# DeltaNet with a GELU MLP: the triangular inverse by 16-row blocks on GpSimd, four-tile products, and planned instruction refills

## The chip, the core and the metric

The kernel runs on one core of one Trainium2 chip. The metric is the device time of a whole execution in microseconds (us), the median of three runs. Five engines work side by side, each through its own list of instructions in order, and tell each other by semaphores when a result is there: TensorE (PE) multiplies matrices, VectorE (DVE) and ScalarE (ACT) work element by element, GpSimd (POOL) does so[...], and SyncE (SP) here only issues transfers (DMA). PE results land in PSUM, which has eight banks here; everything else lies in SBUF, 128 partitions wide.

## What is computed

First a delta-rule recurrence for 4 batches x 8 heads, 768 steps, head width 48; then an MLP on the 3,072 rows of 384 that come out of it.

```python
def _attn_ref(q, k, v, beta):
    k_n = k / (np.linalg.norm(k, axis=-1, keepdims=True) + 1e-06)
    state = np.zeros((B, H, D, D))
    for t in range(S):                       # S = 768
        kt, vt, bt = k_n[:, :, t], v[:, :, t], beta[:, :, t, None]
        y[:, :, t] = einsum('bhd,bhde->bhe', q[:, :, t], state)
        v_old = einsum('bhde,bhd->bhe', state, kt)
        state = state + bt[..., None] * einsum('bhd,bhe->bhde', kt, vt - v_old)
    return y
# x = y as rows (b, s) of all heads: 3072 x 384
h = x @ w_in                                 # 384 -> 2048
g = 0.5 * h * (1 + tanh(c * (h + 0.044715 * h**3)))
return g @ w_out                             # 2048 -> 384
```

A kernel can't afford 768 steps in a row. It takes the sequence in 12 chunks of 64 steps. Inside a chunk the updates depend on each other through a 64x64 triangular matrix per head: with K the normalized keys and N the strictly triangular part of the Gram matrix K K^T scaled by beta, the chunk needs T = (I + N)^-1. Then R = V - K S (S is the state at the chunk's start), U = beta T R, the output is Q S + tri(Q K^T) U, and the next state is S + K^T U. Only this last part runs from chunk to chunk; T of a chunk needs nothing but its keys and beta.

## The kernel before

The program lists operations with their costs and dependencies, a planner in the kernel orders them for each engine when the program is built, and the order is fixed from then on. So what lies beside what is decided by the planner, not by the order of the text. Two heads share the 128 partitions, 16 pairs make the 32 heads; `g` is one of two groups of eight pairs.

```python
def prep(c):                     # ... norms of the keys of chunk c
    sq = k*k; ss = sum(sq)       # POOL or ACT, then DVE
    sr = ss ** 0.5               # ACT Sqrt for c < 3, else POOL pow
    rn = 1/(sr + 1e-6)           # DVE
    KQ[:, 0] = kf * rn           # POOL
    KQ[:, 1] = qf                # POOL or ACT
    KQT = dma_transpose(KQ)      # SP: keys and queries, head width on the partitions
```

(The lines above are shortened to what they do; those below are code, with cuts.)

```python
def intra(c, g):
    def gd():                                     # Gram: K K^T and K Q^T, four tiles
        for mm in range(4):
            for (hh, a) in ((0, 0), (1, 1), (0, 1), (1, 0)):
                ...
                r.append((bank(h, hh)[cc, 128*mm:128*mm+128], KQT[i][rr, 0, m, cc], KQT[i][rr, :, m, cc], ...))
    ... # N = Gram * (mask * beta)   DVE from PSUM;   DT = K Q^T * mask   DVE from PSUM
    ... # W = I + N, Z = I - N       POOL (DVE for c < 2)
    def prod(hx, lhs, rhs):
        def body():
            return [(bank(hx)[64*a:64*a+64, 64*p:64*p+64], lhs[64*a:64*a+64, p, :],
                     rhs[64*a:64*a+64, p, :], True, True, True) for p in range(8) for a in range(2)]
        return f_mms(body)
    ... # X = W^T by 16 PE transposes, evacuated by ACT
    for j in range(5):                            # Newton: Z <- Z (2I - X Z)
        op(..., {"pe": prod(h1, Zo, X)}, ...)
        op(..., {"dve": f_tt(F, bc(twoI), v1(h1), ALU.subtract)}, ...)
        op(..., {"pe": prod(h2, F, Zo)}, ...)
        op(..., {"act": f_act(dst, v1(h2))}, ...)  # last round writes TT

def state(c):
    ... # qs: Q S;  ks: K S                   PE, 32 products each, four tiles
    ... # R = vf - K S                        DVE
    def tr():                                 # T R: 32 products, tile (a, a): two of four tiles
        return [(bank(h2, p//8)[64*a:64*a+64, ...], TT[i][64*a:64*a+64, p, :],
                 R[64*a:64*a+64, p, :], True, True, True) for p in range(NP) for a in range(2)]
    ... # U = beta * T R                      DVE
    ... # ku: K^T U, S = S + K^T U            PE four tiles, DVE
    ... # du: tri(K Q^T) U, added to Q S in PSUM   PE, two tiles
    ... # x = output, two evacuations         ACT

def mlp(t):                                   # tiles of chunks: [0] [1,2] [3,4] ... [11]
    op({"sp": 1.1}, {"sp": f_dma(xT[...], x[...], True)}, ...)     # transposing DMA
    for fc in range(FC):                      # 16 slices of the hidden width
        ... # m1: 3 products, w columns (512, or 256 for one chunk);  gT = gelu   ACT
    for u in range(w // 128):
        ... # m2: 16 products of 384 columns;  osb = PSUM   DVE or ACT;  DMA out
```

Of the kernel before, what the change touches and what calls it, by code (L numbers as in the profile page):

```python
# [6 lines left out]
BF16 = mybir.dt.bfloat16  # L7
ALU = mybir.AluOpType
# [3 lines left out]
C = 64  # L12
# [3 lines left out]
KEEP = 0.0  # L16
BANKS = {"t": (0, 6), "f": (6, 8), "l": (0, 8)}
NEAR = {"pe": 0.3, "dve": 0.05, "act": 0.05, "pool": 0.0, "sp": 0.0}


class Op:
    __slots__ = ("idx", "cost", "fns", "deps", "prio", "alloc", "uses", "dma", "lat",
                 "eng", "start", "end", "count", "clock", "sync", "mode", "bw")


class Plan:
# [14 lines left out]
    def op(self, cost, fns, reads=(), writes=(), prio=0.0, alloc=(), dma=None, lat=0.0, mode="t", bw=0.0):  # L41
        o = Op()
        o.idx = len(self.ops)
        o.cost, o.fns, o.prio, o.dma, o.lat, o.mode, o.bw = cost, fns, prio, dma, lat, mode, bw
        o.alloc = tuple(alloc)
        o.sync = set()
# [8 lines left out]
        for b in writes:  # L55
            if b in self.last_w:
                deps.add(self.last_w[b])
            deps.update(self.readers.get(b, ()))
# [14 lines left out]
    def schedule(self):  # L73
# [16 lines left out]
        pe_mode = "t"  # L90
        dma_free = 0.0
# [5 lines left out]
        def dep_time(o, e):  # L97
            t = 0.0
            for d in o.deps:
                p = ops[d]  # L100
                t = max(t, p.end + (p.lat if p.dma else (0.03 if p.eng == e == "pe" else LAT[p.eng])))
            return t
# [16 lines left out]
        while n_left:  # L119
            pick = None  # L120
            for e in ENGINES:
# [3 lines left out]
                for i in ready[e]:  # L125
# [4 lines left out]
                    bb = []  # L130
                    if o.alloc:
                        ok = True
                        taken = []
                        for h, n in o.alloc:
                            sv = [(k, bank_free[k]) for k in taken]
                            for k in taken:
                                bank_free[k] = None
                            f = find_banks(n, t, *BANKS[o.mode])
                            for k, x in sv:
                                bank_free[k] = x  # L140
                            if f is None:
                                ok = False
                                break
                            bb.append((h, f[1], n))
                            taken += list(range(f[1], f[1] + n))
                            t = max(t, f[2] + 0.15)
                        if not ok:
                            continue
                    late = max(0.0, t - free_at[e])
                    pr = o.prio  # L150
                    if e == "pe" and (o.mode == "t") != (pe_mode == "t"):
                        pr += KEEP
                    far = late > NEAR[e]
                    key = (far, t if far else 0.0, pr, i)
                    if best is None or key < best[0]:
                        best = (key, i, t, bb)
# [6 lines left out]
            _, i, t, bb, e = pick  # L163
            o = ops[i]
            if e == "pe" and (o.mode == "t") != (pe_mode == "t"):
                t += SWITCH
                pe_mode = o.mode
            o.eng, o.start, o.end = e, t, t + o.cost[e]
            if o.dma:
                dma_free = max(o.end + 1.3, dma_free) + o.bw  # L170
                o.lat = dma_free + 0.5 - o.end
# [28 lines left out]
    def emit(self):  # L200
# [21 lines left out]
        for _ in range(len(ops)):  # L222
# [12 lines left out]
            for d in o.deps | o.sync:  # L235
                p = ops[d]
                if p.eng == "pe" and e == "pe" and not p.dma:
# [45 lines left out]

def f_tt(out, a, b, op):
# [27 lines left out]
def d_ps(n):  # L312
    return {"dve": 0.13 + 1.07e-3 * n}


def d_any(n):
    return {"act": 0.18 + 0.83e-3 * n, "dve": 0.13 + 1.07e-3 * n}
# [6 lines left out]
def d_pool2(n):  # L324
    return {"pool": 0.10 + 2.0e-3 * n}


def bass_deltanet__then__act_gelu_tanh_kernel(
# [12 lines left out]
    NP = NH // 2  # L341
    NCH = S // C
    KT = DM // 128
    FC = FF // 128
    TILES = [[0]] + [[c, c + 1] for c in range(1, NCH - 1, 2)] + [[NCH - 1]]
# [7 lines left out]
    with nc.allow_non_contiguous_dma("head rows"), nc.allow_low_precision("bf16 matmuls"):  # L353
# [3 lines left out]

        identF = sb("identF", [128, 128], F32)
        mU128 = sb("mU128", [128, 128], F32)
        idI = sb("idI", [128, 64], F32)  # L360
        mU = sb("mU", [128, 64], F32)
        half = sb("half", [128, NP], F32)
        BL = sb("BL", [128, 3, 2, 64], F32)
        bcol = sb("bcol", [128, NP, NCH], F32)
        RL, RB, NSQ = 3, 3, 3
        identB = sb("identB", [128, 64], BF16)
        twoI = sb("twoI", [128, 64], BF16)
        kf = [sb(f"kf{i}", [128, NP, D], F32) for i in range(RL)]
        qf = [sb(f"qf{i}", [128, NP, D], F32) for i in range(RL)]
        vf = [sb(f"vf{i}", [128, NP, D], F32) for i in range(RL)]  # L370
        sq = [sb(f"sq{i}", [128, NP, D], F32) for i in range(2)]
        ss = [sb(f"ss{i}", [128, NP], F32) for i in range(2)]
        sr = [sb(f"sr{i}", [128, NP], F32) for i in range(2)]
        rn = [sb(f"rn{i}", [128, NP], F32) for i in range(2)]
        KQ = [sb(f"KQ{i}", [128, 2, NP, 64], BF16) for i in range(RB)]
        KQT = [sb(f"KQT{i}", [128, 2, NP // 2, 128], BF16) for i in range(RB)]
        NU = [sb(f"NU{i}", [128, NP, C], F32) for i in range(2)]

        def ring(nm, n, w):
            return [[[sb(f"{nm}{i}{g}{j}", [128, 8, w], BF16) for j in range(n)] for g in range(2)] for i in range(RB)]  # L380

        Nb, Wb, Xb, Zb, Fb = ring("N", 1, C), ring("W", 1, C), ring("X", 1, C), ring("Z", 2, C), ring("F", 1, C)
        DTb = [sb(f"DT{i}", [128, NP, C], BF16) for i in range(RB)]
        TT = [sb(f"TT{i}", [128, NP, C], BF16) for i in range(RB)]
        Rb = [sb(f"R{i}", [128, NP, D], BF16) for i in range(2)]
        Ub = [sb(f"U{i}", [128, NP, D], BF16) for i in range(2)]
        Sb = [sb(f"S{i}", [128, NP, D], BF16) for i in range(2)]
        x = sb("x", [128, 2, B, DM], BF16)
        xT = sb("xT", [128, 2, B * KT, 128], BF16)
        W1 = sb("W1", [128, KT, FF], BF16)  # L390
        W2 = sb("W2", [128, FC, DM], BF16)
        gT = [sb(f"gT{i}", [128, FC, 512], BF16) for i in range(2)]
# [16 lines left out]

        def aff(dst, cmp_, fill, pat, cm):  # L410
            return lambda g: g.affine_select(out=dst, in_=dst, compare_op=cmp_, fill=fill, base=0,
# [6 lines left out]
        op({"dve": 0.1}, {"dve": lambda e: e.memset(half[:, :], 0.5)}, writes=["half"], prio=-100)  # L418
        for i in range(RB):
            op({"dve": 0.7}, {"dve": lambda e, i=i: e.memset(KQ[i][:, :, :, D:64], 0.0)},  # L420
               writes=[f"KQz{i}"], prio=-90 + i)
        const("identF", identF, 0.0, ALU.not_equal, 1.0, [[-1, 128]], 1)
        const("mU128", mU128, 1.0, ALU.is_gt, 0.0, [[1, 128]], -1)
        for nm, big, sm in (("idI", identF, idI), ("mU", mU128, mU)):
            bn = {"mU": "mU128", "idI": "identF"}[nm]
            for a in range(2):
                r = slice(64 * a, 64 * a + 64)
                op({"dve": 0.1}, {"dve": f_cp(sm[r, :], big[r, r])}, reads=[bn], writes=[nm + str(a)], prio=-80)
        MASKU, IDI = ["mU0", "mU1"], ["idI0", "idI1"]
        op({"dve": 0.1}, {"dve": f_cp(identB[:, :], idI[:, :])}, reads=IDI, writes=["identB"], prio=-80)  # L430
        op({"dve": 0.1}, {"dve": lambda e: e.tensor_scalar(twoI[:, :], idI[:, :], 2.0, None, op0=ALU.mult)},
           reads=IDI, writes=["twoI"], prio=-80)

        bulk = []

        def gate():
            return bulk[-2] if len(bulk) > 1 else []

        def load(nm, c, pr):
            t, src = {"kf": (kf, k), "qf": (qf, q), "vf": (vf, v)}[nm]  # L440
            s = c % RL
            sv = src.rearrange("b h s d -> (b h) s d").rearrange("(p a) s d -> a s p d", a=2)
            after = gate()
            for a in range(2):
                op({"sp": 0.65}, {"sp": f_dma(t[s][64 * a:64 * a + 64, :, :], sv[a, C * c:C * c + C, :, :])},
                   reads=after, writes=[f"{nm}{s}_{a}"], prio=pr, dma=f"d_{nm}{c}", bw=1.05)
            bulk.append([f"{nm}{s}_{a}" for a in range(2)])

        w1v = moe_w_in.rearrange("(kt p) f -> p kt f", p=128)
        w2v = moe_w_out.rearrange("(fc p) e -> p fc e", p=128)  # L450

        def load_w(nm, j, pr):
            if nm == "W1":
                dst, src, bw = W1[:, j, :], w1v[:, j, :], 2.9
            else:
                dst, src, bw = W2[:, 4 * j:4 * j + 4, :], w2v[:, 4 * j:4 * j + 4, :], 2.2
            op({"pool": 0.8}, {"pool": f_dma(dst, src)}, reads=gate(), writes=[f"{nm}{j}"], prio=pr,
               dma=f"d_{nm}{j}", bw=bw)
            bulk.append([f"{nm}{j}"])

        STEP = 28.0
# [5 lines left out]
        load("kf", 0, -70)  # L467
        for dup in range(2):
            op({"sp": 0.65}, {"sp": f_dma(BL[:, :, dup, :], bfl)}, writes=[f"BL{dup}"], prio=-69, dma="d_BL", bw=0.4)
        load("qf", 0, -68)  # L470
        load("kf", 1, -67)
        load("qf", 1, -66)
        W1N = [f"W1{kt}" for kt in range(KT)]
        W2N = [f"W2{j}" for j in range(4)]

# [7 lines left out]
        op({"pe": 1.0}, {"pe": f_mms(bt_mms)}, mode="f", reads=["BL0", "BL1", "identF"], writes=[hb_ + (0,), hb_ + (1,)], alloc=[(hb_, 1)], prio=-50)  # L483
        for a in range(2):
            r = slice(64 * a, 64 * a + 64)
            op({"dve": 0.35}, {"dve": f_cp(bcol[r, :, :], lambda a=a, r=r: bank(hb_)[r, 0:NH * NCH].rearrange(
                "q (p a c) -> q p a c", a=2, c=NCH)[:, :, a, :])}, reads=[hb_ + (a,)], writes=[f"bcol{a}"], prio=-49)
        BCOL = ["bcol0", "bcol1"]


        def prep(c):
            s, i, j = c % RL, c % RB, c % 2
            pr = T(c, -STEP)
            kn = [f"kf{s}_0", f"kf{s}_1"]
            parts = [slice(0, 8), slice(8, 16)] if c == 0 else [slice(0, NP)]
            for n, u in enumerate(parts):
# [3 lines left out]
                op(cost, {"pool": f_tt(sq[j][:, u, :], kf[s][:, u, :], kf[s][:, u, :], ALU.mult),  # L500
# [314 lines left out]
```

## Time and profile before

| What | Value |
|---|---|
| Time, median of 3 | 326.49 us (325.32 to 327.86) |
| Profiled span, first to last instruction | 322.0 us |
| PE busy | 272.2 us, 7,158 products |
| DVE, ACT, POOL busy | 175.0, 175.3, 127.1 us |
| Solver products X,Z and Z,F, 64x64 | 1,920 and 1,920 |
| MLP products of 512, 256 and 384 columns | 240, 96 and 384 |
| DVE, F out of PSUM, 120 times | 80.4 us, 684 ns each |
| POOL, square roots by pow, 9 times | 26.2 us, 2,911 ns each |
| Transfers | 31.84 MB in 116,206 packets, 110,640 of them under 512 bytes |
| Mean granted PE clock | 0.945 of full |

How to read it: a row of the profile names the engine, the operation, the output and inputs by the program's names, how often it ran, its busy time and the mean of one. "ps" is any PSUM tile, so "ps<-X,Z" is the first product of a solver round and "ps<-Z,F" the second; "ps<-xT,W" and "ps<-W,gT" are the MLP's two layers. "L301" is only the helper that emits products. Products overlap in PE's pipeline, and the profile's end of a product is modelled; the start of the next one is measured. "issue" in the chain is time in which an engine waited for nothing that the profile shows. q8 is the queue that brings instructions.

### The profile page before, as it was taken

The numbers are of one execution on the slowest core, as the hardware profiler recorded it, in microseconds if no ns is written. First come the engines' busy times: TensorE is split into PE (matmuls) and PEld (weight loads), VectorE is DVE, ScalarE is ACT, GpSimd is POOL, SyncE is SP. The second block draws the span as 40 slices with busy tenths as digits, with TensorE's granted clock in tenths as the row PEclk, the third lists the DMA queues.
The fourth block names the chain that finished last, engine by engine and source line by source line (L and its number), as shares of the span: only waits on it lengthen the run. The fifth ranks groups of instructions, "written<-read, shape, count | busy, mean of one in ns | idle before, by whom it ended". The sixth has DMA issues, their size and how long they took to land.

```text
span 322.0 us, 15234 instructions
## 1 busy us (share of the span) xinstructions
PE 272.2 (85%) x7158; PEld 178.4 (55%) x7158; DVE 175.0 (54%) x279; ACT 175.3 (54%) x309; POOL 127.1 (39%) x96
## 2 busy tenths in 40 slices
PE   1158745988859789999899979989999999989995
PEld 1147644656636466666556556555566556544662
DVE  3489723767557467766775566674556554320111
ACT  4325543668447578634778443777345774168330
POOL 2842330877987257455546371260202211000000
PEclk9998775779998799999999999999999999999999
DMA  7998889879998435495557541709001002101022
GB/s 134 168 182 169 131 119 180 155 151 172 170 176 139 93 69 102 85 181 111 111 100 107 113 103 51 118 4 118 26 29 53 2 9 48 66 36 24 24 75 49
DMA packets 116206, 31.84 MB, mean 99 GB/s; under 512 B 110640, under 2 KB 115760, under 8 KB 116144
## 3 DMA queue, kind: packets, MB, share of 16 engines
q1 hardware_dynamic: 113600, 27.73, 45.5%
q0 software_dynamic: 2544, 3.15, 6.8%
q8 instruction: 56, 0.92, 1.2%
q14 instruction: 6, 0.05, 0.0%
HBM read 20.64 MB, written 4.72 MB: 79 GB/s over the span
## 4 chain that ended last, share of the span: by engine, by line
PE 51%; DMA 22%; issue 7%; DVE 7%; ACT 5%; SPq 4%; POOL 2%; POOLq 0%
PE ps L301 50%; DMA kf<-in_k_dram 8%; DMA qf<-in_q_dram 6%; DMA vf<-in_v_dram 4%; SPq L309 4%; DMA xT<-x 2%; DVE F L285 2%; DMA KQT<-KQ 1%; ACT Z L294 1%; ACT sq L294 1%; ACT x L294 1%; PE ps L600 1%; POOL sr L285 1%; DVE ss L503 1%; DVE R L285 1%
## 5 line engine op out<-in xcount | busy, mean ns | idle before, releaser
L285 DVE TENSOR_TENSOR F<-twoI,ps 128x512 bf16<-128x512 bf16 x120 | 80.4, 684 | 58.4 <-PE ps L301 57.7
L301 PE MATMUL ps<-xT,W 128*128 128x512 bf16 (+1 forms) x336 | 80.6, 364 | 1.8 <-ACT gT L294 1.0
L294 ACT ACTIVATE Z<-ps 128x512 bf16<-128x512 f32 x96 | 56.2, 595 | 42.3 <-PE ps L301 41.5
L294 ACT ACTIVATE gT<-ps 128x512 bf16<-128x512 f32 (+1 forms) x112 | 58.2, 536 | 32.3 <-PE ps L301 31.2
L301 PE MATMUL ps<-W,gT 128*128 128x384 bf16 x384 | 70.0, 327 | 0.6 <-ACT gT L294 0.6
L301 PE MATMUL ps<-X,Z 64*64 64x64 bf16 x1920 | 53.9, 201 | 12.8 <-ACT Z L294 6.9
L301 PE MATMUL ps<-Z,F 64*64 64x64 bf16 x1920 | 54.7, 201 | 8.7 <-DVE F L285 4.0
L301 PEld LDWEIGHTS ps<-X,Z 64*64 64x64 bf16 x1920 | 42.8, 116 | 29.8 <-ACT Z L294 15.1
L301 PEld LDWEIGHTS ps<-Z,F 64*64 64x64 bf16 x1920 | 43.0, 115 | 28.7 <-DVE F L285 15.8
L285 POOL TENSOR_TENSOR W<-identB,N 128x512 bf16<-128x512 bf16 x20 | 23.0, 1151 | 81.8 <-DVE N L285 78.1
L301 PEld LDWEIGHTS ps<-W,gT 128*128 128x128 bf16 x384 | 34.5, 98 | 21.8 <-ACT gT L294 0.8
L301 PEld LDWEIGHTS ps<-xT,W 128*128 128x128 bf16 x336 | 26.7, 100 | 23.1 <-ACT gT L294 4.2
L290 DVE COPY osb<-ps 128x384 f32<-128x384 f32 x20 | 11.1, 557 | 41.3 <-PE ps L301 41.3
L285 POOL TENSOR_TENSOR sr<-ss,half 128x16 f32<-128x16 f32 x9 | 26.2, 2911 | 5.4 <-DVE ss L503 5.2
L285 POOL TENSOR_TENSOR KQ<-kf,rn 128x768 bf16<-128x768 f32 (+1 forms) x12 | 17.1, 1423 | 21.2 <-PE ps L301 16.9
L285 POOL TENSOR_TENSOR NU<-mU,bcol 128x1024 f32<-128x1024 f32 x12 | 23.6, 1971 | 4.4 <-DVE N L285 4.0
L294 ACT ACTIVATE x<-ps 64x768 bf16<-64x768 f32 x24 | 19.3, 804 | 8.2 <-PE ps L301 7.9
L285 POOL TENSOR_TENSOR Z<-identB,N 128x512 bf16<-128x512 bf16 x20 | 23.0, 1151 | 0.0
L294 ACT ACTIVATE TT<-ps 128x512 bf16<-128x512 f32 x24 | 14.3, 596 | 13.4 <-PE ps L301 13.4
L294 ACT ACTIVATE X<-ps 128x512 bf16<-128x512 bf16 x24 | 14.3, 595 | 12.9 <-PE ps L600 12.9
L285 DVE TENSOR_TENSOR N<-ps,NU 128x512 bf16<-128x512 f32 x24 | 16.3, 686 | 8.6 <-PE ps L301 8.6
L301 PE MATMUL ps<-KQT 48*64 48x128 bf16 x384 | 12.7, 246 | 6.6 <-DMA KQT<-KQ 6.4
(49 smaller groups left out, 202.4 us busy)
## 6 DMA issues: line engine op xcount, KB each, us to landing
kf<-in_k_dram SPq DMA_DIRECT2D x24, 192.0 KB, 4.0
qf<-in_q_dram SPq DMA_DIRECT2D x24, 192.0 KB, 3.9
vf<-in_v_dram SPq DMA_DIRECT2D x24, 192.0 KB, 4.3
out_dram<-osb SPq DMA_DIRECT2D x20, 192.0 KB, 1.9
W<-in_moe_w_in_dram POOLq DMA_DIRECT2D x3, 512.0 KB, 6.0
W<-in_moe_w_out_dram POOLq DMA_DIRECT2D x4, 384.0 KB, 7.1
out_dram<-osb SPq DMA_DIRECT2D x8, 96.0 KB, 2.7
BL<-in_beta_dram SPq DMA_DIRECT2D x2, 96.0 KB, 3.6
```

Of the source, the lines that this page charges most:

```text
L285: return lambda e: e.tensor_tensor(out() if callable(out) else out, a() if callable(a) else a, b() if callable(b) else b, op)
L290: return lambda e: e.tensor_copy(out, a() if callable(a) else a)
L294: return lambda e: e.activation(out, a() if callable(a) else a, func)
L301: ins = t.matmul(out, lhsT, rhs, start=st, stop=sp_, skip_group_check=skip)
L309: return lambda e: e.dma_start(out, a)
L503: op({"dve": 0.95 * w}, {"dve": lambda e, u=u: e.tensor_reduce(ss[j][:, u], sq[j][:, u, :], AX.X, ALU.add)}, reads=[f"sq{j}{n}"], writes=[ ...
L600: ins = t.transpose(bankb()[r, p, :], W[r, p, :], identB[r, :])
```

## The change

The new kernel computes the same with another way to T, other layouts, and another planner.

- **T by blocks.** A 64x64 triangle is cut into four 16-row blocks. PE first forms only the four 16x16 diagonal blocks of each Gram matrix (`own`, 64 products of 32x32 per chunk); a DVE transpose brings them to a layout in which each partition holds whole 16x16 blocks, for two chunks at once (a unit). POOL solves them there by substitution: 14 steps of one multiply and one add on short rows (`blocks`; the first unit on DVE). Two DVE transposes return the blocks. `inverse` expands them to block-diagonal matrices (DI, WB), forms E from the Gram matrix and WB in one set of products, and fills the off-diagonal blocks of T in three rounds of products (48, 32, 16 columns). This replaces the 22 sets of 16 solver products and transposes per chunk.
- **All four PE tiles.** In `state`, T R and the product with DT are laid out so that neighbouring products use all four 64x64 tiles (from chunk 2 on for T R). The output comes out transposed, so the MLP's input no longer needs the transposing DMA; rows of the fourth slice are moved by small SBUF to SBUF transfers, and tile 0 uses a fourth weight slice W4 instead.
- **Transposes of K and Q** are done on PE (128 columns each) and evacuated by DVE or ACT. Queries are loaded for two chunks at a time in longer runs.
- **Norms** from chunk 4 on by three Newton steps on DVE, for two chunks together, in place of POOL's pow.
- **MLP tiles** are [0], [1], and then pairs. Weights are loaded by ten POOL-issued transfers for the first layer, behind POOL's start-up work, and four for the second.
- **The planner** models the refill of PE's instructions in blocks of 256 and places bursts so that a refill has time to arrive; priorities are set by a table.

The core of the diff, with cuts:

```diff
+class Fetch:
+    BLOCK, FIRST, EVENTS = 256, 63, 1.0025
+    TIMES = ((50.0, 6.5), (125.0, 4.5), (1e9, 3.7))
+    ...
+                    if e == "pe":
+                        t0 = t + turn(pe_mode, o.mode)
+                        w = o.cost[e] * (COLD if t0 < COLD_T else 1.0)
+                        stall = fetch.run(t0, w, o.nm) - t0 - w
+                        t += max(0.0, stall - SLACK)
...
-    TILES = [[0]] + [[c, c + 1] for c in range(1, NCH - 1, 2)] + [[NCH - 1]]
+    TILES = [[0], [1]] + [[c, c + 1] for c in range(2, NCH, 2)]
...
-            op({"sp": 1.1}, {"sp": f_dma(KQT[i]..., KQ[i]..., True)}, ...)
+                        for m in ms:
+                            ins = e.transpose(tb()[:, m, :], t[:, 2 * m:2 * m + 2, :]..., identB[:, :])
...
+        def own(cs):
+            ...
+                                o = bank(h, hh)[64 * a + 32 * b:64 * a + 32 * b + 32, x_:x_ + 32]
+                                kk = kqt[64 * hh:64 * hh + D, 0, m, a, b, :]
+                                r.append((o, kk, kk, True, True, True))
+        def blocks(cs):
+            eng = "pool" if u else "dve"
+            ...
+            op({"dve": 1.4}, {"dve": lambda e: e.transpose(Tt[j]..., banks2(h)...)}, ...)
+            for s in range(14, 0, -1):
+                w = 15 - s
+                ... # tmp[j, u] = Y[s, u] * Y[j, s]   for w x s elements, two chunks
+                ... # Y[s+1:, 0:s] += tmp
+            ... # XW[0] = Y * beta by rows, XW[1] = Y * beta by columns
+                op({"dve": 1.05}, {"dve": lambda e, w=w: e.transpose(TB1... if w else TB0..., XW[w]...)}, ...)
+        def inverse(c, hs):
+            exp(1, WB[e_], f"WB{e_}", 0)          # DVE (ACT early)
+            exp(0, DI[r_], f"DI{r_}", 0.1)
+            ... # ps = G WB (32 products);  ET = ps * mask
+            for k in (1, 2, 3):
+                n = 64 - 16 * k
+                ... # ps = ET^T src, 32 products of n columns;  TT[:, 16k:] = ps + DI   DVE
-            for j in range(5):
-                ... # Z <- Z (2I - X Z)
...
-                return [(bank(h2, p // 8)[64 * a:64 * a + 64, ...], TT[i][64 * a:64 * a + 64, p, :], ...)]
+                if fl:
+                    return [(bank(h2, p % 2)[HALF[a], D * (p // 2):D * (p // 2) + D],
+                             TT[r_][HALF[a ^ (p % 2)], p, :], R[HALF[a ^ (p % 2)], p, :], True, True, True)
+                            for p in range(NP) for a in range(2)]
+                    r.append((oc(m, hh, a), U[HALF[a], p, :], DTb[r_][HALF[a], p, :], c == 0 and n < 4, True, True))
...
-            op({"sp": 1.1}, {"sp": f_dma(xT[:, s, :, 0:n], x[0:n, s, :, :]..., True)}, ...)
+            for c_ in range(2):
+                for j in range(KT if t else 0):
+                    op({XQ: 0.7}, {XQ: f_dma(xs[64*c_+48:64*c_+64, j, :, 0:n], xs[64*c_+16*j:64*c_+16*j+16, 3, :, 0:n])}, ...)
```

On PE the program order falls from 7,158 products to 5,443; 120 F operations on DVE and 96 Z evacuations on ACT are gone.

## The prediction

> **What bounds the kernel now.** I read the page's busy shares first, then the chain that ended last, then the timeline of TensorE in a steady stretch, because only start-to-start times there tell what a burst of small products really costs.
>
> ```profile
> PE 272.2 (85%) x7158; PEld 178.4 (55%) x7158; DVE 175.0 (54%) x279; ACT 175.3 (54%) x309; POOL 127.1 (39%) x96
> ...
> q8 instruction: 56, 0.92, 1.2%
> ```
>
> TensorE (PE) is the nearest to full; no other engine passes 55%. But 272.2 us is a union of spans whose ends are modelled (201 ns for a 64x64 product that is followed some 16 ns later by the next), so part of it is drain and not work. The chain, in order of time, shows two different kernels:
>
> ```profile
> 10.23 4.70 DMA KQT<-KQ
> ...
> 42.37 4.00 issue
> ...
> 49.25 7.49 DMA xT<-x
> 56.79 1.38 PE ps L301 x13
> ...
> 292.61 25.56 PE ps L301 x165
> ```
>
> Up to 56.8 us it is a latency chain: load, norm, a transposing DMA (4.7 us), five solver rounds of chunk 0, another transposing DMA (7.5 us); only then can the MLP feed PE. Loads stand on the chain again from 87 us (qf 5.00 us, then kf 5.49). The last 26 us are pure MLP. Between, PE is the bound. Its real prices stand in the timeline of the PE rows:
>
> ```profile
> 257.62 0.82 PE L301 MATMUL ps<-xT,W 128*128 128x512 bf16 x3
> 258.37 0.44 PE L301 MATMUL ps<-X,Z 64*64 64x64 bf16 x16
> 258.74 0.82 PE L301 MATMUL ps<-xT,W 128*128 128x512 bf16 x3
> 259.60 0.44 PE L301 MATMUL ps<-Z,F 64*64 64x64 bf16 x16
> 259.87 0.66 PE L301 MATMUL ps<-R,TT 64*64 64x48 bf16 x32
> ...
> 261.59 0.44 PE L301 MATMUL ps<-U,KQ 64*64 64x48 bf16 x32
> 261.86 0.66 PE L301 MATMUL ps<-U,DT 64*64 64x48 bf16 x32
> ...
> 298.79 1.46 PE L301 MATMUL ps<-W,gT 128*128 128x384 bf16 x8
> 300.09 0.49 PE L301 MATMUL ps<-xT,W 128*128 128x256 bf16 x3
> 300.42 1.46 PE L301 MATMUL ps<-W,gT 128*128 128x384 bf16 x8
> ```
>
> Sixteen Z,F products on the two diagonal tiles take 259.87-259.60 = 0.27 us, 17 ns each. Thirty-two U,KQ products on all four tiles take 261.86-261.59 = 0.27 us, 8.4 ns each. U,DT (two tiles, 32), where nothing waits, runs from 62.65 to the next burst at 63.16: 0.51 us, 16 ns, which I use for two tiles. Eight second-layer products take 1.30 us, 162 ns; three 256-column ones 0.33 us, 110 ns; by columns a 512-column one is 217 ns. Three of those are 0.65 us and the small burst starts 0.75 us later: some 0.09 us for a change between MLP and small products.
>
> Sum before: MLP 240x0.217 + 96x0.110 + 384x0.1625 = 125 us. Attention per chunk: 352 solver products and transposes x 16 ns = 5.6; Gram 32x16 ns = 0.5; S,KQT 64x8.4 ns = 0.5; R,TT and U,DT 0.5 each; U,KQ 0.27; together 7.9, times 12 = 95 us. The program order has 224 changes between MLP and small products, x 0.09 = 20 us. Total 240 us, against a PE that ends at 318. So about 78 us is not work: 43 us before 56.8 us (14 of work there), and 35 us after.
>
> In the stretch 112 to 288 us alone the PE groups give 190 and 256 MLP products and 3,744 attention products: 82.8 + 62 + some 15 of changes = 160 of 176 us, 91%.
>
> **The Trainium skill.** "TensorEngine Tiling (Array Packing)", Tiling Modes: 64x64 gives four independent tiles, 32x32 sixteen, and a change of mode drains the array. The trace agrees with both (8.4 against 16 ns; 0.09 us per change). "TensorE: Matmul & The Clock Gate", the aside on 56 ns in Part 1: matmul start-to-start never falls below about 25 ns; the trace differs (8.4 ns on four tiles), and I use the trace. "Runtime: NRT & Kernel Launch", Instruction fetch mechanics: instructions are refilled in blocks of 256. The q8 row agrees: 56 packets, and 2x7158/256 = 55.9. The page calls the cost mostly hidden; the trace shows single "issue" gaps of 4.00 us. "GPSIMD Engine Reference", Elementwise (about 2.6 cycles per element at 1.2 GHz for two inputs) bears on the solver: it would give 1.66 us for 768 elements; in the trace the KQ<-kf,rn products on POOL take 1,477 ns for 768 elements and 827 ns for 384, which is 0.18 us plus 1.69 ns per element.
>
> **The change, part by part.** (1) PE. Removed per chunk: 352 products (5.6 us). Added per chunk: 64 own-block Gram products of 32x32 (at 8.4 ns, an estimate from the four-tile burst, 0.5); 16 transposes of 128 columns for K and Q (by columns 54 ns, 0.9); WB 32x8.4 ns = 0.27; three block rounds of 32 on two tiles, 96x16 ns = 1.5 at most. R,TT moves from two to four tiles (0.5 to 0.27) and so does U,DT, turned round to 64 columns (0.5 to 0.3). With the Gram 0.5, S,KQT twice 0.27 and U,Kn 0.27 a chunk is 5.1, times 12 = 61 us, against 95. MLP gains 16 products of 256 columns (tile 0 takes four contraction slices): 127. The order shows 150 changes for 224: 13.5 against 20. Total 202 for 240: 38 us less work. PE's instructions fall from 7,158 products to 5,443, so 43 refills instead of 56.
>
> (2) Start. Both transposing DMAs leave the first chain. Mine: keys of chunk 1 land about 8 us; norms, scaling, transposes, evacuation, own blocks to about 14.5 (the keys' norm chain before took 5.58 to 9.94); one transpose on VectorE (DVE) of 1,024 elements 1.3; the solve of unit 0 on DVE: 28 dependent small operations at 0.17 to 0.25 (TENSOR_SCALAR and RECIPROCAL of 128x16) plus a handoff, near 0.28, = 8, and four of 512 elements at 0.69; two transposes back: near 28.5. Expansion and block rounds with their DVE and ScalarE (ACT) steps 5; R to U to the output 3.3: x of chunk 0 near 37. But W1 is issued on GpSimd (POOL) only behind its start-up work, which I sum to about 25 us (KQ-sized operations by the rate above), in ten transfers; weight transfers took 6 to 7 us to land on busy queues (the page's DMA issues), so they land 40 to 44. I take the first MLP product at 41 us, against 57.
>
> (3) The solve in steady state. One unit of two chunks on POOL: 28 operations x 0.18 + 2,240 elements x 1.69 ns = 8.8, three 512-element ones at 1.04, and 5 of scaling, squares and masks: 17 us. PE needs per two chunks 20.8 (MLP) + 10 + 2 = 33. POOL lies beside it. DVE per two chunks: I count 26 us (four 0.95, TT 0.95+0.69+0.42, DT two 0.69, DI and output two 0.56 each, reduction 0.94, transposes and norms 2.6, each per chunk). ACT about 25 with its DMA issues. All below 33, so PE remains the bound.
>
> (4) After 41 us: 202 less the 13.5 done by then is 188.5. The order's end is 72+24 first-layer and 64+64 second-layer products without attention: 42 us, dense as the 25.56 us piece is. The other 146.5 I divide by 0.95: before it was 0.91, but loads, transposes and refills are now more out of the way; 154 us. The granted clock fell to 0.5-0.8 between 32 and 72 us before; I add 2.5 us for such a dip. Last evacuation and output as before, 3.8. Span: 41+154+2.5+42+3.8 = 243.3. Time stood 4.5 us above span (326.49 against 322.0): 248 us.
>
> **Rivals.** *The solve becomes the wait*: 28 dependent POOL operations of maybe 0.5 us each with their handoff would make 25 us a unit, still under 33, but the first POOL unit also stands behind the start-up and weight issues; chunk 2 might come after the MLP of tiles 0 and 1 has run out. For it: long in-order POOL list. Against: 39% busy before, and 3 us pow operations (26.2 us in all) are gone. It would add 5 to 15 us: 253 to 263. *DVE and ACT, filled to 80%, stall PE*: before, DVE waited 57.7 us on PE for F and PE only 23.7 for F, at 54% busy; a fuller engine in order gives 0.88 instead of 0.95: 12 us more, 260. *The dense plan works as planned*: efficiency 0.99, start at 37: 234. *The slack eats it*: PE work falls but the recurrence of chunks binds. A state step is about 5 us (four bursts with drain, 0.95+0.95 on DVE, 0.8 on ACT), 60 us in all, so I give it little.
>
> **Range and chances.** The terms with room are the start (37 to 46) and the efficiency (0.88 to 0.99); together about 234 to 266, so the range is 234 to 263. None of the rivals comes near 320: faster by over 2% 0.97, within 0.02, slower 0.01.
>
> **What would show it.** First x,W product near 41 us; PE products 5,443 and 43 instruction packets; PE start-to-start near 8.4 ns in R,TT and WB; no DMA transpose; POOL under 60% with gaps; the final MLP piece 42 us. Wrong if the first MLP product is after 50 us, if PE idles on POOL or DVE for more than 20 us between 60 and 190 us, if 32x32 products cost well over 8.4 ns, or if "issue" gaps stay near 4 us.

## The result, and the profile after

The changed kernel takes 260.25 us (median of 4 runs, 259.79 to 260.78) against 327.0 us before (4 runs): a ratio of 0.797, 95% interval 0.794 to 0.799. I had predicted 248 us, with 234 to 263 as the range. Measured again at a later time, beside runs 9 to 11, the same kernel took 258.82 us; so between two measurements taken at different times, 1.5 us are not read as a difference.

The page of the changed kernel: busy time by engine, the queue of instruction refills, and the chain that ended last by engine.

```profile
PE 216.8 (84%) x5416; PEld 143.3 (55%) x5446; DVE 160.3 (62%) x288; ACT 145.1 (56%) x244; POOL 127.7 (49%) x234
...
q8 instruction: 42, 0.69, 1.2%
...
PE 41%; POOL 28%; DVE 15%; issue 4%; DMA 4%; SPq 3%; ACT 3%; POOLq 0%
```

PE lost 55 us of busy time (272.2 before) and 1,712 products, counted by their weight loads (7,158 to 5,446; 30 product records are missing after). Refills fell from 56 to 42. POOL, 2% of the chain before, is 28% of it now. The DMA share of the chain fell from 22% to 4%: the transposing transfers, 3% of it, are gone, and the loads of k, q and v fell from 18% to 4%.

PE's new prices stand in its timeline. A row gives the start and the duration in us, the engine, line and operation, the output and inputs, the tile of the array, the elements, the type and how many; brackets, where there are any, hold the idle time before it and what ended that.

```profile
68.68 0.65 PE L388 MATMUL ps<-KQT 48*32 48x32 bf16 x64
69.27 0.50 PE L388 MATMUL ps<-x,W 128*128 128x256 bf16 x3
...
76.73 0.67 PE L388 MATMUL ps<-TT,ET 64*64 64x16 bf16 x32
77.34 1.47 PE L388 MATMUL ps<-W,gT 128*128 128x384 bf16 x8
78.74 0.44 PE L388 MATMUL ps<-R,TT 64*64 64x48 bf16 x32
79.01 0.42 PE L388 MATMUL ps<-WB,G 64*64 64x48 bf16 x32
```

Thirty-two R,TT products now take 79.01 - 78.74 = 0.27 us, 8.4 ns each, as U,KQ did before. Sixty-four 32x32 own-block products and the change to the MLP take 0.59 us; less 0.09 for the change, 7.8 ns each. The block rounds on two tiles cost the same whether they stream 48 columns or 16: the 16-column round takes 77.34 - 76.73 = 0.61 us with its change, the 48-column one at 71.11 us takes 0.62.

The end is dense MLP, with no gap:

```profile
204.16 0.44 PE L388 MATMUL ps<-DT,U 64*64 64x64 bf16 x32
204.53 9.27 PE L388 MATMUL ps<-W,gT 128*128 128x384 bf16 x56
213.86 15.49 PE L388 MATMUL ps<-x,W 128*128 128x512 bf16 x70
...
244.98 10.56 PE L388 MATMUL ps<-W,gT 128*128 128x384 bf16 x64
```

The start is not as predicted. These are the rows of PE before the first MLP product that show a gap put down to "issue", and that product itself:

```profile
39.56 0.46 PE L388 MATMUL ps<-DI,ET 64*64 64x48 bf16 x10 [2.83 <-issue]
...
47.26 1.31 PE L388 MATMUL ps<-TT,ET 64*64 64x16 bf16 x43 [4.12 <-issue]
...
53.16 0.37 PE L388 MATMUL ps<-DT,U 64*64 64x64 bf16 x11 [2.31 <-issue]
...
56.50 0.82 PE L388 MATMUL ps<-x,W 128*128 128x256 bf16 x3
```

Three times PE stands still in the middle of a burst and waits for nothing that the profile knows: 9.3 us in all. PE's timeline has 127 recorded products from the first gap to the second and 128 from the second to the third; with a weight load each that is a block of 256 instructions, so the gaps stand where a refill is due. The first MLP product comes at 56.50 us (56.79 before, 41 predicted), so the whole gain of 67 us lies behind it. In two windows of 8 us there, the columns after the busy times of the engines are the granted PE clock, the packets' summed time as a share of 16 DMA engines' time (which can pass 1), and GB/s:

```profile
core 0: us, PE busy (x) PEld busy (x) DVE busy (x) ACT busy (x) POOL busy (x), PEclk, DMA share, GB/s
40.00:48.00 8.00, 3.88 (x148) 3.79 (x146) 5.80 (x10) 3.13 (x5) 6.72 (x17) 0.50 1.24 171
48.00:56.00 8.00, 4.79 (x203) 4.20 (x203) 6.49 (x17) 2.43 (x3) 7.02 (x16) 0.50 1.15 183
```

The transfers are busy all through, with the MLP's weights (POOL issued W1 from 31.5 us, W2 from 36.8 us; their queue is active from 32 to 54 us), and the granted clock is half, until 62 us. A burst of 32 products on two tiles takes 0.95 us here (48.40 to 49.35 us) instead of 0.53 (0.62 at 71.11 us, less 0.09 for the change).

The Trainium skill, "TensorE: Matmul & The Clock Gate", Part 1 (The HAM clock gate), puts a halved clock down to an idle window of about 3.4 us. These traces do not show that. Here the clock fell at about 38.2 us, 1.5 us into the first gap (mean of 0.59 over 38 to 39 us). In run 9 below it fell at about 36.6 us (0.78 over 36 to 37), when its first gap was 0.1 us old. In run 2 it fell at about 44.3 us (0.63 over 44 to 45), amid bursts, with no gap above 0.8 us in the 5 us ahead. So the long gaps are not what the half clock needs; what lowers it is not shown.

### The profile page after: what moved, and what is told of

Same layout as the page of the kernel before. It is cut to its first block, busy times and chain, and to the rows that moved or that the text cites. A ratio compares the mean times of both kernels' runs of the same rounds, so it can differ in the third digit from the quotient of the medians.

```text
span 258.6 us, 11905 instructions
## 1 busy us (share of the span) xinstructions
PE 216.8 (84%) x5416; PEld 143.3 (55%) x5446; DVE 160.3 (62%) x288; ACT 145.1 (56%) x244; POOL 127.7 (49%) x234
## 4 chain that ended last, share of the span: by engine, by line
PE 41%; POOL 28%; DVE 15%; issue 4%; DMA 4%; SPq 3%; ACT 3%; POOLq 0%
PE ps L388 40%; POOL Yf L916 6%; POOL tmp L912 6%; POOL Kn L372 4%; POOL sq L372 4%; SPq L396 3%; POOL W L396 3%; DMA qf<-in_q_dram 2%; DVE TB L936 2%; DVE WB L979 2%; DMA kf<-in_k_dram 2%; POOL DT L372 2%; POOL Yf L907 1%; ACT gT L381 1%; DVE TT L372 1%
## 5 line engine op out<-in xcount | busy, mean ns | idle before, releaser
L381 ACT ACTIVATE gT<-ps 128x512 bf16<-128x512 f32 x96 | 55.6, 597 | 40.0 <-PE ps L388 37.9
L388 PE MATMUL ps<-x,W 128*128 128x512 bf16 (+1 forms) x306 | 67.4, 353 | 4.5 <-issue 2.5
L388 PEld LDWEIGHTS ps<-x,W 128*128 128x128 bf16 x336 | 29.9, 99 | 24.6 <-ACT gT L381 1.0
L372 DVE TENSOR_TENSOR TT<-ps,DI 128x256 bf16<-128x256 f32 (+4 forms) x39 | 24.9, 644 | 13.1 <-PE ps L388 12.6
L381 ACT ACTIVATE KQT<-ps 128x1024 bf16<-128x1024 bf16 (+1 forms) x24 | 23.6, 984 | 12.9 <-PE ps L795 10.6
L916 POOL TENSOR_TENSOR Yf<-Yf,tmp 128x28 f32<-128x28 f32 (+6 forms) x70 | 24.6, 351 | 5.5
L912 POOL TENSOR_TENSOR tmp<-Yf 128x28 f32<-128x28 f32 (+6 forms) x70 | 23.8, 340 | 5.4
L388 PE MATMUL ps<-KQT 48*32 48x32 bf16 (+1 forms) x1152 | 20.1, 207 | 6.8 <-DVE tmp L912 2.9
L372 POOL TENSOR_TENSOR Kn<-kf,rn 128x768 bf16<-128x768 f32 (+1 forms) x12 | 17.0, 1429 | 8.9 <-DVE rn L737 7.0
L388 PE MATMUL ps<-TT,ET 64*64 64x32 bf16 (+1 forms) x768 | 17.9, 182 | 4.2 <-issue 4.1
L381 ACT ACTIVATE x<-ps 128x1024 bf16<-128x1024 f32 x12 | 12.3, 1021 | 6.9 <-PE ps L388 6.6
```

What stands on the lines that cost most here:

```text
L372: return lambda e: e.tensor_tensor(out() if callable(out) else out, a() if callable(a) else a, b() if callable(b) else b, op)
L381: return lambda e: e.activation(out, a() if callable(a) else a, func)
L388: ins = t.matmul(out, lhsT, rhs, start=st, stop=sp_, skip_group_check=skip)
L912: sb_op(nb * s * w, lambda e, s=s, w=w, tv=tv: e.tensor_tensor(tv, yf[:, :, s:s + 1, 0:s].to_broadcast([128, nb, w, s]), Yv()[:, :, s + 1: ...
L916: sb_op(nb * s * w, lambda e, s=s, tv=tv: e.tensor_tensor(Yv()[:, :, s + 1:16, 0:s], Yv()[:, :, s + 1:16, 0:s], tv, ALU.add), [YN, f"tmp{j ...
```

## Experiments

**Theory.** The start is late because PE's instruction packets queue behind the weight transfers. **Rivals.** The chain of small steps is simply that long; or POOL's solve, 28% of the chain of waits, sets the time. The first four runs move the weights, take the refill plan away, and take four-tile products back.

### 1. W2 issued later

```diff
 after the planner has fixed the orders:
+w2 = [i for i in po if P.ops[i].dma[:4] == "d_W2"]     # po: POOL's list
+po[:] = [i for i in po if i not in w2]
+po[79:79] = w2                                         # behind the solve of unit 1
```

> The order of every engine stays; only the four second-layer weight transfers move in GpSimd's list from before its first solve (issued 36.8 to 39.9 us) to behind it. Theory 'refills wait behind the weights': of the three refill gaps of TensorE before the first MLP product (2.8, 4.1, 2.3 us) the last two shrink to under 1 us each, the first MLP product comes at 50 to 53 us instead of 56.5, and the time falls 2 to 5 us, to 255 to 258. Rival 'the chain of the first chunks itself is too long': first MLP product within 1 us of 56.5, time within 1 us of 260.2. Rival 'the wait is for the first-layer weights': no change of the first MLP product either.

Measured: 265.7 us, ratio 0.818 (0.813 to 0.823), slower than the kernel after. The start did move: gaps of 2.54, 3.02 and 0.58 us, the third one nearly gone, and the first MLP product at 53.62 us. But PE then stood still for 5.77 us:

```profile
72.28 0.69 PE L388 MATMUL ps<-KQT 48*32 48x32 bf16 x64 [5.77 <-DVE ET L372]
```

DVE's ET waited for DI, and DI for the transfer that swaps the halves of TB. SyncE's timeline of the same run shows why this came late:

```profile
66.12 1.90 SPq L396 DMA_DIRECT2D qf<-in_q_dram  x2
68.07 1.18 SPq L396 DMA_DIRECT2D TB<-TB  x2
```

The swap was issued at 68.07 us (58.72 in the kernel after), behind a load of q that is made to wait for W2's transfers as a pacing measure. What was moved was not only W2 but whatever waits for it in another list.

### 2. W1 early and W2 late

The six W1 transfers, the two of W4 and the two of W1x move to the 19th place of POOL's list (they were issued from 19.3 us), W2 as in 1.

> As the one before, and the ten first-layer weight transfers move in GpSimd's list from 31.5 us to ahead of its norms of chunks 2 and 3 (about 16 us). Refill theory: all three gaps shrink, together under 3 us instead of 9.3; first MLP product near 48 us; time 252 to 256. Rival 'chain too long': no more than 1 us of change. What could spoil it: the weights then slow the loads of 16 to 30 us and hold GpSimd 5 us earlier, so norms of chunks 2 and 3 are later.

Measured: 270.64 us, ratio 0.834 (0.829 to 0.838).

```profile
43.38 0.34 PE L388 MATMUL ps<-DI,ET 64*64 64x48 bf16 x10 [0.79 <-issue]
...
48.16 1.30 PE L388 MATMUL ps<-TT,ET 64*64 64x16 bf16 x43 [0.91 <-issue]
...
59.21 0.82 PE L388 MATMUL ps<-x,W 128*128 128x256 bf16 x3
```

The same two gaps, at the same instructions, are 0.79 and 0.91 us and the third is absent: 1.7 us where the kernel after has 9.3. That fits the weight traffic as the cause of most of the gap time. But PE reached these bursts some 6 us later, which gave the refills more time as well, and this run doesn't part the two. The time went up nonetheless: issuing W1 took 5.4 us of POOL's list before the norms of chunks 2 and 3, and PE's list has the transposes of these keys ahead of the block rounds of chunks 0 and 1. They came 5.9 us later (30.80 and 36.36 us for 24.92 and 30.49), so the chain arrived later than the gaps gave back, and the stall of 1 came again (5.68 us at 78 us).

### 3. No refill plan

```diff
     def run(self, t, cost, n, keep=False):
+        return t + cost
```

The planner no longer reckons with refills; everything is planned anew.

> The planner places TensorE's operations without its model of refills (a run costs its cost); all else is the changed kernel. If planned refills are worth what their place in the change says, the issue gaps on TensorE grow from 12 us in all to 18 or more and the time rises 3 to 8 us, to 263 to 268. Rival 'TensorE meets the same refills in any order': within 1.5 us of 260.2.

Measured: 272.32 us, ratio 0.836 (0.830 to 0.842): 12 us slower than the kernel after, more than expected. So the plan that reckons with refills carries a sixth to a fifth of the whole gain of 67 us. PE's waits that are put down to "issue" sum to 12.2 us in the kernel after; in this run (us in sum, times, longest):

```profile
PE ps L389 <- issue: 20.5, 31, 2.9
```

So some 8 of the 12 us are such gaps; the rest was not traced. (The profiles of this run and of solve_on_dve below come from executions in a slower state, 3 to 4 us longer than the others of the same kernel, so their sums are read to a few us only.)

### 4. Two tiles instead of four

```diff
-            fl = int(c > 1)
+            fl = 0            # R,TT and WB,G on two tiles; v is loaded unflipped
```

> The products R,TT and WB,G go back to two of four tiles in every chunk (layouts with them), the planner knows it. By my prices (16 ns against 8.4 ns a product) 20 bursts of 32 cost 0.24 us more each: 4.9 us, time 265. Rival 'TensorE has 10% slack, so it costs nothing': within 1 us of 260.2. Rival 'the planner's new order is what changes': anything, shown by gaps elsewhere.

Measured: 266.55 us, ratio 0.821 (0.816 to 0.826), so 6.3 us more by the medians.

```profile
78.39 0.69 PE L388 MATMUL ps<-R,TT 64*64 64x48 bf16 x32
78.91 0.66 PE L388 MATMUL ps<-WB,G 64*64 64x48 bf16 x32
```

A two-tile R,TT burst took 0.52 us (0.27 in the kernel after), so the 20 bursts of chunks 2 to 11 give up 5.0 us. PE's busy time rose by 4.7 us (221.5 for 216.8) and its idle time by 0.5, so what PE gives up appears in the time. It is not POOL that makes the end later: its solves of units 4 and 5 begin at 132.46 and 160.60 us, ahead of the kernel after (137.79 and 163.38). Yet the order was planned anew, and a part of its own for the new order is not excluded.

### 5. W2 not loaded

```diff
-POOL: W2[:, 4j:4j+4, :] <- dma(w_out)
+POOL: W2[:, 4j:4j+4, :] <- memset(constant)      # same place in the list
```

This leaves out the load of the second layer's weights; all orders stay.

> The second-layer weights are not loaded: GpSimd fills W2 with a constant at the place in its list where it issued the four transfers, so 1.57 MB less goes through the DMA between 37 and 54 us; all orders stay. Output is then not the reference's. Theory (the start is late because instruction packets of TensorE queue behind the weight transfers): the three gaps of 2.83, 4.12 and 2.31 us sum to 4 to 6.5 instead of 9.3, the first x,W product comes at 52 to 54.5 us instead of 56.5, the time is 255 to 258.5 us. Rival (the start is long because of the chain of small products and expansions itself, and the gaps lie in it anyway): first x,W within 1 us of 56.5, time 259 to 261.5.

Measured: 259.86 us, ratio 0.795 (0.789 to 0.801).

```profile
38.76 0.46 PE L388 MATMUL ps<-DI,ET 64*64 64x48 bf16 x10 [2.06 <-issue]
...
45.63 1.31 PE L388 MATMUL ps<-TT,ET 64*64 64x16 bf16 x43 [3.29 <-issue]
...
49.62 0.37 PE L388 MATMUL ps<-DT,U 64*64 64x64 bf16 x11 [0.39 <-issue]
...
54.96 0.82 PE L388 MATMUL ps<-x,W 128*128 128x256 bf16 x3
```

The gaps sum to 5.7 us and the third goes, as the refill theory says. The first product would have come earlier still, but S on DVE now held PE up by 2.20 us. And the time is that of the rival: the start gained 1.5 us and the end nothing that can be told from 0.

### 6 and 7. W2 late, with SyncE freed of the wait

```diff
 as 1, and
+for i in P.orders["sp"]:
+    if P.ops[i].dma:
+        P.ops[i].deps -= w2s      # loads no longer wait for W2; no data passes between them
```

> As w2_late (W2 issued behind the solve of unit 1), and the loads of q in SyncE's list no longer wait for the W2 transfers, so that the swap of TB's halves, which stands behind them in that list, is not held up. Theory (w2_late lost because TB's swap was issued at 68.1 instead of 58.7 us): no stall of TensorE at 66 to 72 us, first x,W at 52.5 to 55, time 255.5 to 259. Rival (late W2 costs by itself, its traffic meeting the loads of q and v and the second-layer products): 261 to 266 us with TensorE idle at 62 to 80 us.

Measured: 258.72 us, ratio 0.793 (0.784 to 0.801). PE's stall at 66 to 72 us is gone, so SyncE's list accounts for what 1 lost (7 us by the medians). First MLP product at 54.04 us. The same with the four transfers spread through POOL's solve:

> As w2_late_freed, with the four W2 transfers issued one at a time through the second half of unit 1's solve (about 46, 50, 54 and 58 us) instead of together behind it. Theory: instruction packets wait for less of a queue than in the kernel after, more than in w2_late_freed: gaps of 5 to 8 us in sum, first x,W at 53 to 56, time 256 to 260. Rival (any W2 traffic before the first MLP product costs as much as all of it): gaps 9 us, first x,W at 56 to 57.5, time 259.5 to 262.

Measured: 260.36 us, ratio 0.797 (0.791 to 0.802); gaps 2.65 and 2.75 us, no third, the first product at 54.03 us. Like no_w2_load: earlier start, and no difference in the time that the medians show. The profiles show how far the lead goes. In runs 5 and 6 POOL's solve of unit 2 begins at 72.29 and 72.57 us and that of unit 5 at 161.77 and 161.69, against 74.04 and 163.38 us in the kernel after (73.48 and 163.50 when measured again), and the spans are 257.6 and 256.9 us against 258.6 and 258.8. In run 7 unit 5 begins at 163.19 us and the span is 258.8. So 1 to 2 us of the lead may reach the end, or none; single profiles can't settle it. The start also scatters by itself: in run 8 below and in two_tiles, where the weights are as in the kernel after, the gaps sum to 7.4 and 8.1 us and the first product comes at 54.47 and 55.17 us. What is firm is the third gap, in the runs that keep PE's order at the start: 2.2 to 2.3 us in all with W2 in its place, 0.6 or less in all without.

### 8. The solve of unit 1 made longer

Each of the 14 steps does two extra multiplies into scratch, for unit 1 only.

```diff
-    e.tensor_tensor(tv, yf_bc, Y_bc, ALU.mult)
+    for t in ([scratch, tmp_other] if u == 1 else []) + [tv]:
+        e.tensor_tensor(t, yf_bc, Y_bc, ALU.mult)
```

> GpSimd's solve of unit 1 does two extra multiplies into scratch in each of its 14 steps, some 9.5 us more; nothing else changes. Theory (TensorE's chain sets the start; the solve of unit 1 was ready about 4 us before its second transpose back was wanted): first x,W unchanged within 1 us of 56.5, time +3 to +6.5 us. Rival (GpSimd's solve is what the start and the time wait for, as its 28% of the chain of waits says): +8.5 us or more, all of it.

Measured: 265.33 us, ratio 0.813 (0.805 to 0.820), 5 to 6.5 us above the kernel after. The solve of unit 1 grew from 18.15 to 26.34 us, 8.2 us, and DVE had waited 3.96 us for something else before it took the result. So two or three of the 8.2 us were slack, about as expected.

### 9. The solves of units 2 to 5 made longer

The same edit with `u > 1`.

> The two extra multiplies per step as in pool_slower_unit1, now in units 2 to 5 and not in unit 1: some 38 us more of GpSimd in all. Theory (GpSimd's solve of these units lies beside TensorE's work with room to spare, 82 of 148 us busy; only part of it shows, by less slack and by VectorE standing still more often): +2 to +9 us. Rival (the solve is the chain that the mixed stretch runs on): +25 to +38 us.

Measured: 294.50 us, ratio 0.910 (0.906 to 0.914), against 258.82 us for the kernel after beside it: 35.7 us more. The four solves grew from 16.0 us on average to 24.1, 32.7 us in sum; the order of every engine is as it was. **All of it shows, and my theory falls.** I had expected 2 to 9 us. PE, DVE and POOL of this run, each from its own timeline, at the solve of unit 2:

```profile
89.03 0.83 PE L388 MATMUL ps<-x,W 128*128 128x256 bf16 x6
98.13 1.03 PE L796 MATMUL ps<-identB,Kn 128*128 128x128 bf16 x8 [8.28 <-POOL Kn L372]
```

```profile
95.23 1.04 DVE L941 STREAM_TRANSPOSE TB<-XW 128x512 f32<-128x512 f32 x1 [7.01 <-POOL XW L933]
```

```profile
94.14 1.06 POOL L933 TENSOR_TENSOR XW<-Yf,nbT 128x512 f32<-128x512 f32 x1
95.15 1.49 POOL L928 TENSOR_TENSOR XW<-Yf,nbT 128x512 f32<-128x512 f32 x1
96.61 1.47 POOL L372 TENSOR_TENSOR Kn<-kf,rn 128x768 bf16<-128x768 f32 x1
```

PE waits for more than the inverse. The normalized keys Kn of the next chunks stand behind the solve in POOL's list, and PE's list has their transposes at a fixed place. From the first MLP product to the dense end PE's recorded waits for POOL and DVE grew from 2.2 us to 32.6 us. POOL's gaps in the kernel after (81 of 148 us busy) are no slack in this order: up to its last solve it waits 19.4 us for DVE and 12.8 us for loads of q and k, and a part of what DVE does there is work on POOL's previous solve. The chain of waits of the kernel after, in order of time from unit 3's solve to unit 4's, shows this loop:

```profile
104.03 1.29 POOL Yf L907
...
117.61 1.07 POOL XW L928
118.70 1.08 DVE TB L936
...
123.81 2.01 DVE WB L979
...
127.09 2.14 DVE WB L979
...
134.50 0.36 DVE rn L737
...
134.93 2.91 POOL Kn L372 x2
137.84 1.25 POOL Yf L907
```

From 104 to 153.8 us the chain never touches PE: POOL solves (14.6 us up to the end of the first of its two XW), DVE takes 16.2 us for transposes, expansions, the state's sums and the norm, POOL goes on. All the same PE waited only 2.2 us for the two in that kernel. So the run shows that the solve has no room to grow in this order. It doesn't show that a shorter solve would save time, nor what a plan made for the longer solve would lose; neither was tried.

### 10. The kernel after once more, and two expansions on ScalarE

> The kernel after once more, unchanged, beside the next one. Every theory: 259 to 261.5 us; gaps of TensorE ahead of the first x,W product 7 to 9.5 us in sum.

Measured: 258.82 us (257.45 to 260.80), ratio 0.799 (0.795 to 0.803), gaps of 3.07, 3.57 and 2.31 us.

Between 80 and 104 us DVE is busy 23.04 of 24 us in the kernel after, so the next edit takes two of its operations away, on top of w2_late_freed:

```diff
+wb = the two WB expansions of unit 2 (DVE, L979)
+P.orders["dve"] loses them;  P.orders["act"][107:107] = wb
```

> As w2_late_freed, and the two expansions WB of unit 2 (chunks 4 and 5; 1.69 and 1.93 us on VectorE there, beside GpSimd's operations) are done by ScalarE, in its idle stretch of 4.7 us at 97 us. Theory (between 80 and 104 us VectorE is the full engine, in part because its operations with two SBUF inputs stand still while GpSimd works): TensorE's wait of 2.0 us for DT at 99 us goes, the time is 256 to 258, 1 to 3 us less than w2_late_freed. Rival (TensorE has other work for that while, or ScalarE is then late with G): within 1 us of w2_late_freed, 258 to 260.

Measured: 258.75 us, ratio 0.798 (0.794 to 0.801): no difference. DVE did become free, and PE's wait of 2.0 us for DT at 99 us fell to 0.4 (its waits for TT rose from 0.6 to 2.7). But DVE's list then met an operation that could not start, as its timeline shows,

```profile
100.26 0.95 DVE L711 TENSOR_REDUCE ss<-sq 128x16 f32<-128x768 f32 x1 [1.97 <-POOL sq L372]
101.13 1.24 DVE L897 STREAM_TRANSPOSE Tt<-ps 128x1024 f32<-128x1024 f32 x1
```

and POOL's:

```profile
98.77 1.47 POOL L372 TENSOR_TENSOR sq<-kf 128x768 f32<-128x768 f32 x1 [3.70 <-DMA kf<-in_k_dram]
```

The time won on DVE was handed to a load of k. Tt, the input of the next solve, starts at 101.13 us, against 101.29 us in w2_late_freed. A wait took the place of the one removed.

### 11. Every solve on DVE

The engine of `blocks` is DVE in every unit, and the order is planned anew; only unit 0 keeps an operand in PSUM, as before.

> The solve of every unit on VectorE instead of GpSimd, planned anew. Theory (VectorE, already at 160 of 258 us, becomes the full engine of the mixed stretch): VectorE busy 205 to 225 us, time 266 to 280 us. Rival (GpSimd's solve costs VectorE as much in standing still as it saves, so the engine is no matter): within 2 us of the kernel after.

Measured: 274.29 us, ratio 0.846 (0.842 to 0.850). DVE's busy time is 195 us, less than I expected, POOL's 61 us. As expected the step to GpSimd is worth its place, some 14 to 15.5 us in this kernel.

No version measured here is shown to beat the kernel after.

## Why the prediction came out as it did

The sum by the prediction's own terms, from the trace of the kernel after: start 56.50 (41 predicted); PE's mixed stretch with the 56 second-layer products that begin the dense part 148.0 + 9.3 = 157.3 (154 + 2.5); the rest of the dense end 41.7 (42); last output 3.1 (3.8); time above span 1.65 (4.5). Together 260.25. Of the 12.3 us of error the start is +15.5 and the last term -2.85; the other three together are less than 1. That the range of 234 to 263 held the result is in part luck: the start lies 10 us outside the 37 to 46 that I had allowed it.

Where the gain came from, by the prediction's prices (an estimate): PE's work fell by 38 us (240 to 202). What is not work fell from 78 us to some 54 (PE ends at 255.5 us), and none of that before the first MLP product, where it is 43 us in both kernels. Of the parts, runs 3, 4 and 11 take back 12, 6 and 14 to 15.5 us, not necessarily to be added; the way by blocks itself, the largest saving of PE's work, was not taken back alone.

**PE's work: right.** The four-tile and 32x32 prices held, 42 refills for 43 foretold, and taking two of the four-tile savings back cost about what the bursts say (6.3 us for 5.0).

**The start: wrong.** "I take the first MLP product at 41 us": I had listed 50 us as what would prove it wrong. Two parts failed. First, "near 28.5" for the end of the second transpose back: it was 33.6 us. The DVE transpose of the own blocks began 2.5 us later than I had it (16.99 for 14.5), the first two 512-element operations took 1.43 and 1.08 us instead of 0.69 each (1.1), a reciprocal in DVE's list waited 0.87 for ScalarE (1.0 with its own time), and WB was put between the two transposes (0.5). Second, "expansion and block rounds 5; R to U to the output 3.3": that took until the x of chunk 0 at 54.65 us, 21 us instead of 8.3. Issue gaps are 9.3 us of it. Of these, W2 makes the third, 2.3 us; the weights together make at most 7.6 (run 2 leaves 1.7, but PE comes later there). Half clock in bursts is another part, whose size was not measured alone. I had noted single gaps of 4 us before and even asked for them as a sign; I put no time for them into the start, because I counted refills (43 for 56) and not where they fall. In this stretch a refill is not hidden, but shows 2.3 to 4.1 us each.

**Whether the end follows the start: open.** My sum adds the start to everything after it. Runs 5 to 7 brought the first product 1.5 to 2.5 us forward and the time by no more than the 1.5 us that measurements at different times differ by, which is too little to say yes or no. How much a start at 41 us would have given the end is not settled: no run reached it.

**"POOL lies beside it": wrong, as far as it meant room to spare.** The duration was too small: the 17 us a unit were 11.9 for the solve and 5 for scaling, squares and masks, and the solve alone took 16.0. A step took about 0.35 us plus 0.07 to the next (0.315 foretold), and with the rest POOL was busy some 20 us a unit. That is still below PE's 33. The step from there to "beside" failed: in run 9 each added microsecond of POOL is in the time. The rival "the solve becomes the wait" had the place right and the reason not quite: what fills is the loop POOL, DVE, POOL, not POOL's list alone, and not the start-up. That its 253 to 263 holds the result is luck, since the miss lies in the start; my own sign for it, PE idle on POOL or DVE for over 20 us, did not come (2.2 us).

**The mixed stretch: right in size, for half the reason.** With recorded products by their prices PE did 120 us of work there, some 4 in records that are missing, and 13 in changes: 137 of 148 us, 93% where I had said 95%. I read that as PE bound. Runs 4 and 9 say that neither PE nor the loop of POOL and DVE has room in this order. That the planner made it so, by filling PE with MLP products, is my reading and was not tested.

**DVE as the full engine: half right.** I had it at 26 us of 33 and gave 0.88 a chance. It is full at 80 to 104 us (96%) and at 118.7 to 134.9 us (97%), between the two solves shown in 9. Relieving it in the first place moved the wait to a load (run 10); the second was not tried. My figure for PE's wait for F before, 23.7 us, adds the waits of its weight loads (19.7) and of its products (4.0), which lie over one another.

## What to carry to other kernels

When a planner has packed the engines' lists, a gap in one of them is not slack: lengthen the operation by a known amount and see how much of it arrives, before saying that it lies beside other work. Count instruction refills by where they fall, not only how many: three of them next to large transfers cost 2.3 to 4.1 us each here. And before moving a transfer, look through the other queues for what waits on it.

## What I had not expected of the hardware

An operation of DVE can take several times as long while POOL works, if both read SBUF. DVE's timeline of the kernel after at four places:

```profile
87.65 1.00 DVE L372 TENSOR_TENSOR nw<-sr,ss 128x32 f32<-128x32 f32 x1
88.69 1.42 DVE L736 TENSOR_SCALAR nw<-nw 128x32 f32<-128x32 f32 x1
...
127.01 2.22 DVE L979 TENSOR_TENSOR WB<-TB,mB 128x768 bf16<-128x768 f32 x1
...
134.28 0.18 DVE L736 TENSOR_SCALAR nw<-nw 128x32 f32<-128x32 f32 x1
```

and POOL's at the same times:

```profile
87.55 1.06 POOL L928 TENSOR_TENSOR XW<-Yf,nbT 128x512 f32<-128x512 f32 x1
88.56 1.50 POOL L923 TENSOR_TENSOR XW<-Yf,nbT 128x512 f32<-128x512 f32 x1
...
126.79 1.62 POOL L372 TENSOR_TENSOR sq<-kf 128x768 f32<-128x768 f32 x1 [1.79 <-DMA kf<-in_k_dram]
```

The 32-element operation that takes 0.18 us with POOL idle (134.28) takes 1.42 us at 88.69 and ends at 90.11, as POOL's XW ends at 90.06; the one before it ends at 88.65, and POOL's at 88.61. The WB at 127.01 ends 0.82 us after POOL's sq (128.41); with POOL idle it took 0.92 us in all. The Trainium skill, "SBUF — State Buffer", Who interferes with whom, says that a DVE instruction with two SBUF inputs contends with a GpSimd instruction that reads SBUF, that one in a two-port mode contends with GpSimd as well, and that the one issued second is blocked for the other's whole instruction. The trace agrees. Moving the solve to GpSimd makes more such meetings: in the mixed stretch the nine WB took 1.30 us on average, so 3.4 us in sum above 0.92 each, and two of these stand on the chain of waits above. In run 11, with the solves on DVE, the eight WB after 100 us took 0.94 to 0.96 us each. The small solve steps of unit 0 on DVE keep one operand in PSUM and took 0.15 to 0.28 us beside a busy POOL. That a PSUM operand in WB would free the loop was not tried.
